# An annealed emission order with convolution taps on GpSimd, in a kernel of linear attention and a gated convolution FFN

## The chip, the cores and the metric

One core of one Trainium2 chip. The time is the device time of one execution in microseconds (us), the median of several runs; the profiled span is the part of it that the trace covers. PE is TensorE's matmuls, PEld its weight loads, DVE is VectorE, ACT ScalarE, POOL GpSimd, SP the engine that here only issues transfers.

## The reference

```python
batch, n_heads, seq, head_dim = (8, 8, 576, 64)      # d_model 512, d_ff 1024, kernel 3
kv = np.einsum('bhsd,bhse->bhde', k, v)
out = np.einsum('bhsd,bhde->bhse', q, kv)
x = out / np.sqrt(np.mean(out * out, axis=-1, keepdims=True) + 1e-06) * g_norm   # -> (B, S, 512)
h = np.maximum(x @ w_in, 0.0)                        # (B, S, 1024)
conv = sum(conv_w[k] * shifted(h, k) for k in range(3))   # depthwise along the sequence
y = (h * sigmoid(conv)) @ w_out
```

## The kernel before

All work is described as a list of small operations with their dependences. The program, before it emits anything, simulates this list with 250 random perturbations and emits the best order found. The batches are handled in five groups, `(0,), (1,), (2, 3), (4, 5), (6, 7)`. The FFN has the layout (channel on partitions, sequence on the free axis); a "tap" multiplies one row of channels of h by a factor that differs per partition, a column of `cw_rel`; an "edge" copies the first column of each sequence, on ACT; an "add" adds shifted taps, on DVE; a "gate" multiplies h by the sigmoid.

```python
def tap(j, ...):                                   # j = 0: left neighbour, 2: right one
    nc.vector.tensor_scalar_mul(
        cst["t"][:, f - f0, :], g.h[:, f, :], cw_rel[:, j, f:f + 1])
def edge(...):                                     # first column of each sequence
    nc.scalar.activation(cv[:, :, :1], hv[:, :, :1], AX.Copy)
def add(j, ...):                                   # three tensor_adds on DVE: conv = h + shifted tap,
    ...                                            # then conv += shifted second tap
def sigmoid(f, ...):
    nc.scalar.activation(cst["c"][:, f - f0, :], cst["c"][:, f - f0, :], AX.Sigmoid,
                         scale=cw_rel[:, 1, f:f + 1])
def gate(...):
    nc.vector.tensor_mul(hs, hs, cst["c"])
...
t0.append(plan.op("DVE", t_cost, tap, 0, deps=relu + t0[:1] + [ratio_done]))
ed = plan.op("ACT", 0.25, edge, deps=h_all)
a0 = plan.op("DVE", a_cost, add, 0, deps=t0 + [ed])
t2 = [plan.op("DVE", t_cost, tap, 2, deps=[a0]) for tap, _ in taps]
a2 = plan.op("DVE", a_cost, add, 1, deps=t2)
Hold(r_tap, t0[0], [a2])          # one tap tile: taps, add, taps, add, one after the other
```

Only batch 0 has its convolution on PE, as matmuls with diagonal matrices (`C_PE = (1, 0, 0, 0, 0)`).

The loads are issued by GpSimd: batch 0 in two halves, w_in, batch 1, w_out, then k, v and q of each later batch, each once its buffer (two batches back) is free. The results leave on SP's queue through `outp = pool("outp", 3)`, three output tiles.

Of the kernel before, what the change touches and what calls it, by code (L numbers as in the profile page):

```python
# [64 lines left out]

BY_ACT = (1, 1, 1, 0, 0)
Q_DMA = (0, 0, 0, 0, 0)
R_DMA = (0, 0, 0, 1, 1)
C_PE = (1, 0, 0, 0, 0)
NORM_TABLES = "natural_log_exp_and_others"  # L70
NF = 4
# [7 lines left out]

# [4 lines left out]
class Hold:  # L84
    def __init__(self, ring, first, last):
        self.ring, self.first, self.left = ring, first, len(last)
        first.takes.append(self)
        for op in last:
            op.gives.append(self)


class Op:
    def __init__(self, at, engines, cost, fn, args, deps):
        self.at, self.engines, self.cost, self.fn, self.args = at, engines, cost, fn, args
        self.kind = fn.__name__ if fn else ""
        self.deps = sorted({d.at for d in deps})
        self.takes, self.gives, self.users = [], [], set()
        self.group = self.engine = None
        for d in deps:
            d.users.add(at)  # L100


class Plan:
# [4 lines left out]

    HOP = 0.2
    ROUNDS = 250  # L110
# [4 lines left out]
    def op(self, engines, cost, fn, *args, deps=()):  # L115
        engines = engines if isinstance(engines, tuple) else (engines,)
        cost = cost if isinstance(cost, tuple) else (cost,) * len(engines)
        o = Op(len(self.ops), engines, cost, fn, args, deps)
        o.group = self.group
        self.ops.append(o)  # L120
        return o

    def run(self, places, back=False):

        ops, n = self.ops, len(self.ops)
        deps = [sorted(o.users) for o in ops] if back else [o.deps for o in ops]
        users = [o.deps for o in ops] if back else [sorted(o.users) for o in ops]
        left = [len(d) for d in deps]
        free, held = {}, {}
        if not back:  # L130
            for o in ops:
                for h in o.gives:
                    held[h], free[h.ring] = h.left, h.ring.free
        ready = sorted((places[i], i) for i in range(n) if not left[i])
        busy, end, eng, order = {}, [0.0] * n, [None] * n, []
        events, waiting = [0.0], []
        while events:
            now = heapq.heappop(events)
            while waiting and waiting[0][0] <= now + 1e-6:
                _, i, kind = heapq.heappop(waiting)  # L140
                if kind:
                    bisect.insort(ready, (places[i], i))
                    continue
                if not back:
                    for h in ops[i].gives:
                        held[h] -= 1
                        free[h.ring] += held[h] == 0
                for u in users[i]:
                    left[u] -= 1
                    if not left[u]:  # L150
                        at = max([now] + [end[d] + (0.0 if eng[d] in ops[u].engines else self.HOP)
                                          for d in deps[u]])
                        heapq.heappush(waiting, (at, u, 1))
                        heapq.heappush(events, at)
            started = []
            for item in ready:
                o = ops[item[1]]
                e = next((e for e in o.engines
                          if e == "LAND" or busy.get(e, 0.0) <= now + 1e-6), None)
                if e is None or not back and any(free[h.ring] < 1 for h in o.takes):  # L160
                    continue
                if not back:
                    for h in o.takes:
                        free[h.ring] -= 1
                end[o.at] = busy[e] = now + o.cost[o.engines.index(e)]
                eng[o.at] = e
                order.append(o.at)
                started.append(item)
                heapq.heappush(waiting, (end[o.at], o.at, 0))
                heapq.heappush(events, end[o.at])  # L170
            for item in started:
                ready.remove(item)
        return (max(end) if len(order) == n else float("inf")), end, eng, order

    def passes(self, places, count):
        best = (float("inf"),)
        for _ in range(count):
            got = self.run(places)
            if got[0] < best[0]:
                best = got  # L180
            if got[0] == float("inf"):
                break
            span, end, _, _ = self.run([-e for e in got[1]], back=True)
            places = [span - e for e in end]
        return best

    def order(self):
        ops = self.ops
        way = [0.0] * len(ops)
        for o in reversed(ops):  # L190
            way[o.at] = min(o.cost) + self.HOP + max((way[u] for u in o.users), default=0.0)
        best = self.passes([-w for w in way], 8)
        rnd = random.Random(1)
        for _ in range(self.ROUNDS):
            width = rnd.choice((1, 2, 4, 8))
            each, shift = rnd.random() < 0.7, {}
            places = [e - min(o.cost) + (rnd.gauss(0, width) if each else
                                    shift.setdefault((o.group, o.kind), rnd.gauss(0, width)))
                      for o, e in zip(ops, best[1])]
            got = self.passes(places, 2)  # L200
            if got[0] <= best[0]:
                best = got
        for o, e in zip(ops, best[2]):
            o.engine = e
        return [ops[i] for i in best[3]]


class Group:
    def __init__(self, n, bs, S):
        self.n, self.bs, self.G, self.T = n, bs, len(bs), S * len(bs)  # L210
        self.kv, self.qT, self.sq = {}, {}, {}
        self.n_o = 0
# [3 lines left out]
def kernel(  # L216
# [53 lines left out]
    for lo in (0, H // 2):  # L270
        for name, src in (("k", k), ("v", v), ("q", q)):
            load(0, name, src, lo, lo + H // 2)
            if lo == 0 and name == "v":
                make_identity(nc, ident)
    w_in_sb = consts.tile([P, n_hd, D_ff], BF16, name="w_in_sb")
    for fs in (slice(0, D_ff // 2), slice(D_ff // 2, D_ff)):
# [3 lines left out]
    def load_batch(b):  # L280
        for name, src in (("k", k), ("v", v), ("q", q)):
            load(b, name, src)

    load_batch(1)
    w_out_sb = consts.tile([P, n_ff, D_model], BF16, name="w_out_sb")
    nc.gpsimd.dma_start(out=w_out_sb, in_=moe_w_out.rearrange("(f p) m -> p f m", p=P))
# [26 lines left out]

    rows = ident.rearrange("p (t m) -> p t m", m=SM)
    neg = consts.tile([P, 2], FP32, name="neg")
    for w in range(2):
        nc.vector.tensor_reduce(neg[:, w:w + 1], rows[:, :, 8 * (w + 1):], mybir.AxisListType.XY,
                                AL.add, negate=True)

# [19 lines left out]

    def dve(n, rate):  # L340
        return 0.16 + n * rate * 0.00104
# [10 lines left out]
    def product(g, bi, t):  # L352

        ps = two_banks("ot_ps")
        for i in range(2):
# [9 lines left out]
    def attention(g):  # L365
# [3 lines left out]
        for bi, b in enumerate(g.bs):  # L369
            kv_done, free_k, free_q = [], [], []  # L370
            hs = H // 2 if first else H
            outs, tr_done, trs = [], None, []
            for h0 in range(0, H, hs):
                st = {}

                def kv_mm(bi=bi, b=b, h0=h0, st=st, n=hs // 2):
                    k_sb, v_sb = qkv["k", b], qkv["v", b]
                    st["ps"] = ps = one_bank([P, n, D], FP32, "kv_ps")
                    for hp in range(n):
                        for r in range(R):  # L380
                            for i in range(2):
                                h = h0 + 2 * hp + i
                                nc.tensor.matmul(  # L383
                                    ps[i * D:(i + 1) * D, hp, :],
                                    k_sb[:, h, r * D:(r + 1) * D], v_sb[:, h, r * D:(r + 1) * D],
                                    start=(r == 0), stop=(r == R - 1))

                def kv_out(bi=bi, h0=h0, st=st, n=hs // 2):
                    if h0 == 0:

                        g.kv[bi] = attn.tile([P, n_hd, 2, D], BF16, name="kv_sb", bufs=6)
                    for i in range(2):
                        for half in range(2):
                            dst = g.kv[bi][half * D:(half + 1) * D, h0 // 2:h0 // 2 + n, i, :]
                            move(st["op"], dst, st["ps"][i * D:(i + 1) * D, :, :])

                mm = plan.op("PE", 1.35 * hs / H, kv_mm,
                             deps=[loaded["k", b, h0], loaded["v", b, h0]] + g.need_kv[bi])
                st["op"] = ev = plan.op(EITHER, 4 * act(hs * 32), kv_out, deps=[mm] + kv_done[:1])
# [3 lines left out]
                if g.by_dma:  # L403
# [5 lines left out]
                    t_issue = plan.op("SP", 1.0, tr, deps=[loaded["q", b, h0]] + g.need_qT[bi])  # L409
                    tr_done = plan.op("DMA", 4.5, None, deps=[t_issue])  # L410
# [466 lines left out]
```

## Time and profile before

| | before |
|---|---|
| time, median of 4 runs (with the changed kernel) | 219.26 us (218.53 to 220.64) |
| profiled span, mean granted PE clock | 215.6 us, 0.971 |
| 1152-element taps on DVE | 48 of 532 ns |
| first h matmul, first output matmul | 23.3 us, 54.8 us |

The busy shares, the clock, the DMA row and the windows are shown in the prediction. Two more lines are needed. First the page's chain that ended last, the share of the span by engine; the chain of before ends where it meets an unbroken run of PE, so it explains only the last 60 us:

```profile
PE 26%; ACT 1%; issue 0%; DVE 0%; ACTq 0%
```

Second, two groups by form (operation, partitions x elements, count, busy us, mean ns of one). The first is the DVE tap; the second is the only one-input arithmetic that GpSimd did in this kernel, in fp32, a step of a Newton iteration:

```profile
L670 DVE TENSOR_SCALAR tap<-h,cw_rel 128x1152 bf16<-128x1152 bf16 x48 | 23.8, 532 | 5.6 <-ACT h L621 4.6
...
L496 POOL TENSOR_SCALAR tmp<-tmp 128x288 f32<-128x288 f32 x6 | 4.0, 662 | 0.5
```

### The profile page before, as it was taken

To read this page: it belongs to the slowest core of one execution; us is meant where nothing else is said; L and a number is where in the kernel's file an instruction comes from. 1 tells how busy PE (TensorE), PEld (TensorE's weight loads), DVE (VectorE), ACT (ScalarE), POOL (GpSimd) and SP (SyncE) were. 2 spreads that over 40 slices of the span, in tenths; PEclk is the share of its full clock that TensorE was granted. 3 is DMA by queue.
4 is the path that set the end of the run, shared out by engine and by line. 5 is a ranking of instruction groups with operands and counts; after the bars stand their busy time and mean duration, and the time that the engine had idled before them with its cause. 6 is when DMAs were issued, how large, how long until landed. Compare 5 with 4: busy or idle time off the path is not lost. (4 is left out here: it accounts for less than half of the span.)

```text
span 215.6 us, 4371 instructions
## 1 busy us (share of the span) xinstructions
PE 182.1 (84%) x1742; PEld 111.4 (52%) x1753; DVE 153.2 (71%) x266; ACT 145.5 (68%) x235; POOL 43.1 (20%) x60
## 2 busy tenths in 40 slices
PE   1363898969999697997999999498899999997991
PEld 0341475757657433685554677253447765443440
DVE  2096527688789769867988699999969899972000
ACT  2274169887798969579994468849469798744331
POOL 7841021122120310980003840000000000000000
PEclk9999999999999759999999999889999999999997
DMA  4999999999999999122994108911552101554553
GB/s 61 192 205 205 204 206 204 204 203 205 202 225 224 204 204 210 33 73 82 216 235 135 27 27 201 220 21 49 144 148 61 41 1 51 146 146 128 153 155 99
DMA packets 31575, 30.99 MB, mean 144 GB/s; under 512 B 2092, under 2 KB 26948, under 8 KB 31556
## 3 DMA queue, kind: packets, MB, share of 16 engines
q0 software_dynamic: 20960, 16.25, 48.7%
q1 hardware_dynamic: 10596, 14.47, 26.4%
q8 instruction: 13, 0.21, 0.4%
q14 instruction: 6, 0.05, 0.1%
HBM read 37.24 MB, written 9.73 MB: 218 GB/s over the span
## 5 line engine op out<-in xcount | busy, mean ns | idle before, releaser
L610 PE MATMUL h_ps<-xT,w_in_sb 128*128 128x288 bf16 x512 | 70.8, 295 | 4.2 <-ACT h L621 3.3
L734 PE MATMUL o_ps<-w_out_sb,h 128*128 128x512 bf16 (+1 forms) x285 | 68.2, 386 | 4.2 <-ACT o_sb L346 1.2
L610 PEld LDWEIGHTS <-w_in_sb 128*128 128x128 bf16 x512 | 50.4, 101 | 20.9 <-issue 5.6
L621 ACT ACTIVATE h<-h_ps 128x576 bf16<-128x576 f32 x52 | 33.3, 649 | 23.7 <-PE h_ps L610 23.3
L734 PEld LDWEIGHTS <-h 128*128 128x128 bf16 (+1 forms) x296 | 28.4, 100 | 37.6 <-issue 5.6
L346 ACT ACTIVATE o_sb<-o_ps 128x512 f32<-128x512 f32 (+1 forms) x34 | 20.2, 596 | 24.9 <-PE o_ps L734 22.1
L696 ACT ACTIVATE conv<-conv,cw_rel 128x1152 bf16<-128x1152 bf16 (+1 forms) x32 | 34.4, 1128 | 0.2
L670 DVE TENSOR_SCALAR tap<-h,cw_rel 128x1152 bf16<-128x1152 bf16 (+1 forms) x64 | 29.4, 495 | 5.7 <-ACT h L621 4.6
L444 ACT ACTIVATE sq<-ot_ps 128x576 bf16<-128x576 f32 x32 | 19.7, 653 | 5.0 <-PE ot_ps L358 3.7
L701 DVE TENSOR_TENSOR h<-h,conv 128x1152 bf16<-128x1152 bf16 (+2 forms) x15 | 21.4, 1434 | 2.0 <-ACT conv L696 1.8
L691 DVE TENSOR_TENSOR conv<-h,tap 128x1152 bf16<-128x1152 bf16 (+8 forms) x33 | 20.8, 683 | 0.3
L693 DVE TENSOR_TENSOR conv<-conv,tap 128x1152 bf16<-128x1152 bf16 (+8 forms) x33 | 20.1, 665 | 1.0
L422 PE MATMUL qT_ps<-ident,q_sb 96*128 96x96 bf16 x192 | 13.8, 222 | 4.3 <-ACT kv_sb L346 2.3
L346 ACT ACTIVATE kv_sb<-kv_ps 64x256 bf16<-64x256 f32 (+1 forms) x32 | 11.2, 351 | 8.8 <-PE kv_ps L383 8.5
L348 DVE COPY qT<-qT_ps 128x576 bf16<-128x576 bf16 x20 | 8.8, 454 | 10.9 <-PE qT_ps L422 10.8
L358 PE MATMUL ot_ps<-qT,kv_sb 64*64 64x288 bf16 x192 | 14.2, 318 | 1.9 <-ACT sq L444 0.9
L549 DVE SCALAR_TENSOR_TENSOR xT<-ot_ps,g_sb,rb 128x576 bf16<-128x576 f32 x16 | 12.8, 813 | 4.0 <-PE ot_ps L358 3.8
L623 DVE TENSOR_SCALAR h<-h_ps 128x576 bf16<-128x576 f32 x12 | 9.0, 755 | 8.0 <-PE h_ps L610 7.9
L422 PEld LDWEIGHTS <-q_sb 96*128 96x128 bf16 x192 | 10.9, 106 | 7.1 <-issue 3.1
L581 DVE TENSOR_TENSOR xT<-o,rb_ps 128x576 bf16<-128x576 f32 x16 | 11.2, 747 | 2.6 <-PE rb_ps L573 2.6
L383 PE MATMUL kv_ps<-v_sb,k_sb 96*64 96x64 bf16 x384 | 8.9, 208 | 4.3 <-DMA v_sb<-in_v_dram 4.3
L264 POOL DMA_DIRECT2D k_sb<-in_k_dram x9 | 7.0, 780 | 25.5 <-PE kv_ps L383 19.6
(61 smaller groups left out, 132.6 us busy)
## 6 DMA issues: line engine op xcount, KB each, us to landing
out_dram<-o_sb SPq DMA_DIRECT2D x24, 192.0 KB, 2.3
rb<-scr SPq DMA_DIRECT2D x16, 288.0 KB, 6.6
k_sb<-in_k_dram POOLq DMA_DIRECT2D x7, 576.0 KB, 13.9
v_sb<-in_v_dram POOLq DMA_DIRECT2D x7, 576.0 KB, 16.0
q_sb<-in_q_dram POOLq DMA_DIRECT2D x7, 576.0 KB, 15.7
out_dram<-o_sb SPq DMA_DIRECT2D x24, 128.0 KB, 2.3
out_dram<-o_sb SPq DMA_DIRECT2D x24, 64.0 KB, 2.0
w_in_sb<-in_moe_w_in_dram POOLq DMA_DIRECT2D x2, 512.0 KB, 11.6
```

The costliest lines, as they stand in the source:

```text
L346: nc.scalar.activation(dst, src, AX.Copy, scale=1.0 if scale is None else scale)
L358: nc.tensor.matmul(ps[i * D:(i + 1) * D, e, :HS], g.kv[bi][es, t, i, :], g.qT[bi][es, 2 * t + i, :], start=True, stop=True)
L422: nc.tensor.transpose(ps[:, i, j * PS:(j + 1) * PS], q_sb[:, 2 * t + i, j * P:(j + 1) * P], ident[:PS, :PS])
L444: nc.scalar.activation(g.sq[bi, t], ust["ps"][:, :, :HS], AX.Square)
L610: nc.tensor.matmul(ps[:, e, :HS], w_in_sb[:, t, f * P:(f + 1) * P], g.xT[:, t, at:at + HS], start=(t == 0), stop=(t == n_hd - 1))
L621: nc.scalar.activation(dst, st["ps"][:, :, :HS], AX.Relu)
L670: nc.vector.tensor_scalar_mul(cst["t"][:, f - f0, :], g.h[:, f, :], cw_rel[:, j, f:f + 1])
L691: nc.vector.tensor_add(c[:, :, here], h[:, :, here], t[:, :, there])
L693: nc.vector.tensor_add(c[:, :, there], c[:, :, there], t[:, :, here])
L696: nc.scalar.activation(cst["c"][:, f - f0, :], cst["c"][:, f - f0, :], AX.Sigmoid, scale=cw_rel[:, 1, f:f + 1])
L701: nc.vector.tensor_mul(hs, hs, cst["c"])
L734: nc.tensor.matmul(st["ps"][:n, :], g.h[:, f, t0:t0 + n], w_out_sb[:, f, :], start=(f == 0), stop=(f == n_ff - 1))
```

## The change

The intent: replace the search in the program by a list found by annealing outside (operation number, engine as a letter: `a` ACT, `d` DVE, `p` GpSimd; `*n` adds n matmuls that only keep the clock warm), let that search place the taps on GpSimd too, bring batch 0 in faster, and take work off PE.

```diff
-Q_DMA = (0, 0, 0, 0, 0)
-C_PE = (1, 0, 0, 0, 0)
+Q_DMA = (0, 0, 0, 0, 1)              # q of batches 6, 7 transposed by DMA
+C_PE = ((0, 0, 0, 0), (0, 0), ...)   # no convolution on PE
+TAPS = ("DVE", "POOL")
+PARTS = (3, 1)                       # batch 0: three head pairs, then one
+ORDER = """
+    122 8 7 4 6 5 14*5 15a 16 0 9 26 ... 57p 59 60p 219 61d 69d ... 84p 379 85p ...
+    ... (685 entries)
+"""
 ...
     def order(self):
-        ...                           # 250 rounds of simulation
+        for entry in ORDER.split():
+            entry, _, fill = entry.partition("*")
+            o = self.ops[int(entry.rstrip("adp"))]
+            o.engine = {"a": "ACT", "d": "DVE", "p": "POOL"}.get(entry[-1], o.engine)
+            o.fill = int(fill or 0)
+            yield o
 ...
-                    nc.vector.tensor_scalar_mul(
+                    eng = nc.gpsimd if cst[j, f].engine == "POOL" else nc.vector
+                    eng.tensor_scalar_mul(
                         cst["t"][:, f - f0, :], g.h[:, f, :], cw_rel[:, j, f:f + 1])
 ...
-                nc.scalar.activation(cv[:, :, :1], hv[:, :, :1], AX.Copy)
+                nc.gpsimd.tensor_copy(cv[:, :, :1], hv[:, :, :1])
 ...
-            t_cost = dve(g.T, 0.25)
+            t_cost = 0.215 + g.T * 0.00026
 ...
+                cst[0, f] = op = plan.op(TAPS, (t_cost, 2.3 * t_cost)[:len(TAPS)], tap, 0,
+                                         deps=relu + t0[:1] + [ratio_done])
```

Cut here: the fp32 spread matrix of batch 0's normalization (`spread32`), the kv matmuls of the other order, loads of w_in and w_out in halves placed by the list (w_in now after batch 1, w_out after batch 5), and `tails`, which writes the two 64-row output tiles of batches 0 and 1 into one. The search's price for a tap on GpSimd: 2.3 times DVE's, which is 2.3 x (0.215 + 1152 x 0.00026) = 1.18 us at 1152 elements.

## The prediction

> **What bounds the kernel now.** I read the page's busy shares first, then the chain that ended last, then a table of windows, and last the timeline where PE loses time. Busy shares do not decide it: no engine is full.
>
> ```profile
> PE 182.1 (84%) x1742; PEld 111.4 (52%) x1753; DVE 153.2 (71%) x266; ACT 145.5 (68%) x235; POOL 43.1 (20%) x60
> ...
> PEclk9999999999999759999999999889999999999997
> DMA  4999999999999999122994108911552101554553
> ```
>
> The chain gives the price of PE's work. It runs back over 60 us through PE alone, and matmuls stand end to end there, so a duration divided by its count is a true rate:
>
> ```profile
> 162.87 11.76 PE h_ps L610 x96
> ...
> 178.32 1.73 PE o_ps L734 x8
> 180.04 0.98 PE h_ps L610 x8
> ...
> 194.84 1.25 ACT conv L696
> ...
> 196.12 0.77 DVE h L701
> ```
>
> So an h matmul (288 columns) costs 0.1225 us and an o matmul (512 columns) 0.216 us; the last two lines are the one hole of the tail, the wait for the last sigmoid and gate. At such rates all matmuls (the small ones priced by columns, kv as 48 in 0.79 us, four "product" matmuls as 0.14 us) come to about 156 us; the span is 215.6. PE is the bound, but 60 us of the span are not its work: some 20 at the start, 4.4 after the last matmul, and the rest are losses between. The windows tell where (columns: PE, PEld, DVE, ACT, POOL busy, clock, DMA share, GB/s):
>
> ```profile
> 26.00:70.00 44.00, 40.71 (x608) 29.36 (x606) 31.57 (x59) 35.85 (x60) 8.73 (x12) 1.00 1.30 209
> 70.00:85.00 15.00, 12.07 (x117) 5.65 (x112) 11.45 (x26) 13.13 (x24) 2.81 (x4) 0.77 1.31 204
> 85.00:130.00 45.00, 42.72 (x457) 28.11 (x459) 36.67 (x52) 32.23 (x55) 19.67 (x24) 1.00 0.44 106
> 130.00:145.00 15.00, 11.91 (x82) 8.33 (x82) 14.79 (x20) 11.24 (x16) 0.00 (x0) 0.89 0.73 158
> 145.00:190.00 45.00, 43.62 (x275) 24.54 (x277) 41.02 (x66) 35.10 (x50) 0.00 (x0) 1.00 0.29 78
> ```
>
> Until about 86 us the loads saturate the DMA queue (share over 1, 205 GB/s, the nines of the DMA row). Pricing the matmuls that start in each stretch, PE does 32 us of work in 26 to 70 (0.72 per us, though busy 93%), 7 in the 15 us of the second row, 39 in the third, 10 in the fourth, 42 in the fifth. After 70 us 117 us of work take 141: 24 lost. Of these the clock took 0.23 x 15 + 0.11 x 15 = 5.1, the tail's hole 2.6, and one stall 2.9:
>
> ```profile
> 132.67 4.69 ACT L696 ACTIVATE conv<-conv,cw_rel 128x1152 bf16<-128x1152 bf16 x4
> ...
> 137.95 5.75 PE L610 MATMUL h_ps<-xT,w_in_sb 128*128 128x288 bf16 x32 [2.93 <-ACT h L621]
> ```
>
> Four sigmoids in a row keep ACT from the relu that empties PSUM. The other 13 us are many short waits, DVE being 82 to 99% busy there.
>
> **What the Trainium skill says.** "SBUF — State Buffer", section "Who interferes with whom": VectorE and GpSimd share a port pair under an exclusive lock; a DVE operation in a two-port mode, or with two SBUF inputs against a GpSimd operation that reads SBUF, and the GpSimd operation block each other, whichever is second waiting. The trace agrees: GpSimd's tensor_tensor takes 0.79 us at the median and 1.79 at most, both long ones under a DVE operation of two SBUF inputs, and a DVE tap of 0.53 us took 1.07 at 93.49 us, while GpSimd multiplied. "GPSIMD Engine Reference", section "Engine selection": one-input elementwise work is roughly at line rate there. The trace has only fp32 of 288 elements, 0.433 us at the least. "TensorE: Matmul & The Clock Gate", Part 1: the clock is halved after an idle window of about 3.4 us and restored by sustained work. The trace shows slow matmuls at the start (four h matmuls in 1.12 us at 23.3, eight in 1.14 later); the half clock at 73 us came with PE busy, which this does not explain, so I can't rule it out after the change.
>
> **The change part by part.** I compared the order of instructions on each engine in both builds.
> 1. Convolution of batch 0 leaves PE: 64 matmuls, 13,808 columns, at 0.1225 / 288 per column = 5.9 us off PE. Three diag builds (3.5 us) leave DVE. In their place: 16 more taps, and 24 adds of batch 0, 8 x (0.455 + 0.352 + 0.253) = 8.5 us on DVE; ACT sigmoids are 8 x 0.12 longer.
> 2. The two half-filled output tiles of batches 0 and 1 become one in two column halves: 8 x 0.216 = 1.7 us off PE if the halves run side by side.
> 3. q of the last two batches is transposed by DMA: 48 PE transposes at about 0.043 = 2.1 us off PE, 8 copies of 0.45 = 3.6 us off DVE. It happens long before it is needed.
> 4. Batch 0 is normalized in parts (three head pairs, then one), with an fp32 spread: no split (1.7 us on DVE), but fp32 matmuls at an estimated 0.5 us each, 8 of them, and 10 filling matmuls to warm the clock. All this is before 26 us, where PE was busy 10.6 of 21 us: no cost, but also little gain, since w_in is now loaded after batch 1. By the 2.95 us that each 576 KB load takes at 205 GB/s: batch 0 at 14.3, batch 1 at 23, w_in at 26 and 31. The first h matmul moves from 23.3 to about 26; batch 1 comes 5 us sooner.
> 5. w_out is now loaded after batch 5: 14.3 + 15 x 2.95 + 2 x 2.7 + 5.1 = 69 us. The first output matmul moves from 54.8 to about 69; by then PE does all h of batches 0 and 1 and attention up to batch 5, 29 us of work in 43, the rate of before.
> 6. 38 of 80 taps go to GpSimd, with the edge copies (2.5 us off ACT). DVE saves 19 x 0.53 + 19 x 0.38 = 17 us of them. GpSimd at about 1.15 ns an element (0.433 less 0.1 fixed, over 288) takes 19 x 0.76 + 19 x 1.42 = 41 us beside DVE. Some two thirds of DVE's time then is lock-taking work (taps, adds, gates), so I put the waits at 0.4 us a tap, 15 us: DVE's saving is nearly all given back.
> 7. ACT: three table loads fewer (3.9 us), 5 relus, 2 scalings, 3 evictions and several kv copies fewer: about 14 us off.
> 8. The order: PE's runs are fewer (119 groups against 151), and ACT's late sigmoids stand one or two at a time between relus, not by fours.
>
> Sum for PE: -9.7 us after 26 us, of which the convolution's share lies before 70. At 69 us the new order still has 115 us ahead (288 full o matmuls 62.3, 384 h 47.0, small ones 6), where before had 117 at 70. So the first 70 us gain 1 to 2 us, and the rest must come from the losses. Of 24 us I expect 17: clock 4, tail's hole 3, no sigmoid stall, short waits 10 by the better order, lock waits included. 69 + 115 + 17 + 4.4 = 205.5 us of span. Timed runs were 1.019 times the profiled span (219.6 / 215.6): 209; I say 208, ACT's relief added.
>
> **The rivals.** (a) The lock wins: each tap on GpSimd holds up an add or a gate for a microsecond, DVE (already 99% busy in 130 to 145) becomes the bound with 108 us of own work after 70 plus 20 to 30 of waits, and little is left: 215 to 220. For it: the stretched operations above. Against: many DVE operations there read PSUM and need no lock, and the short taps are early. (b) The late w_out starves PE: GpSimd both issues loads and runs taps in order, so a tap waiting for a relu delays a load; each us of DMA gap before 69 moves the end by one: 212 to 216. Against: most loads are issued a load or two ahead. (c) The order works as found, small waits fall to 5 us and the clock holds: 198 to 202. (d) The kv matmuls now do six on one column half before the other; if they no longer pair, seven batches cost up to 0.5 us more each, 3 us, mostly before 70.
>
> **Range and chances.** (c) sets the low end, (b) with part of (a) the high one: 200 to 217, middle 208. Under 215.2 is faster by over 2%: 0.83. Within 2%: 0.14, if the lock or the loads take all. Slower: 0.03.
>
> **What would show it.** Right: no c_ps group; first o_ps at 66 to 71 us; DMA nines unbroken until about 86; PE busy some 170; DVE busy 155 to 170, adds and gates longer than before (1.38 and 2.55 us at full size); GpSimd busy about 85; ACT about 131; no PE wait over 2 us on a relu after 100. Wrong: the chain running through DVE adds or GpSimd taps (rival a), DMA gaps before 70 (b), or a second long half-clock stretch.

## The result, and the profile after

| | before | after |
|---|---|---|
| time, median of 4 runs | 219.26 us (218.53 to 220.64) | 274.37 us (272.72 to 275.52) |
| ratio, 95% interval | | 1.250 (1.241 to 1.259) |
| profiled span, mean PE clock | 215.6 us, 0.971 | 273.7 us, 0.869 |
| first h matmul, first output matmul | 23.3, 54.8 us | 30.6, 89.4 us |

The changed kernel is 25% slower. A ratio, here and below, is the mean time of one kernel's fast runs over that of the other's in the same rounds, so not quite the ratio of the medians quoted. The sets of runs were not all on the same chip, and the kernel before had medians from 217.98 to 220.33 us in them; ratios are compared, not times of different sets.

The changed kernel's page: busy us and share of each engine, then the clock, the DMA engines' busy tenths and their GB/s in 40 slices (of 6.8 us here), then the chain by engine:

```profile
PE 203.0 (74%) x1696; PEld 118.6 (43%) x1707; DVE 165.7 (61%) x265; ACT 133.3 (49%) x206; POOL 155.7 (57%) x114
...
PEclk9999998687685699999779999577779977997799
DMA  6999909949999499669540009834000210541255
GB/s 91 203 202 205 149 1 149 198 60 203 174 164 199 91 160 203 112 166 222 143 111 7 0 22 219 205 89 143 0 0 2 77 38 4 148 117 34 83 154 153
...
POOL 31%; DVE 27%; PE 22%; DMA 8%; issue 7%; ACT 2%; DVEq 0%; POOLq 0%; ACTq 0%
```

Every engine but GpSimd has a lower share of busy time than before: nobody is full, and the chain goes through GpSimd and DVE (58% together) instead of PE. The clock drops repeatedly: it was at half speed for 71.7 us in sum, against 12.7 before (2.4 of these after the last matmul). Eight of its ten drops come during or after an idle stretch of PE of 3.1 to 10.8 us; the two at 59 and 66 us come with PE 71% and 84% busy in the 6.8 us before, and stay unexplained. And the DMA engines, which before ran at 205 GB/s almost to 86 us, have a hole at 34 to 41 us (149, 1, 149).

The changed kernel's taps by form (the last part of a line is the idle time of the engine just before, and what ended it):

```profile
L746 POOL TENSOR_SCALAR tap<-h,cw_rel 128x1152 bf16<-128x1152 bf16 x19 | 68.1, 3590 | 41.4 <-DVE conv L769 18.2 <-DVE conv L767 15.3 <-ACT h L695 7.9
L746 POOL TENSOR_SCALAR tap<-h,cw_rel 128x576 bf16<-128x576 bf16 x19 | 35.0, 1845 | 16.0 <-DVE conv L767 12.8 <-DVE conv L769 1.9 <-issue 1.1
...
L746 DVE TENSOR_SCALAR tap<-h,cw_rel 128x1152 bf16<-128x1152 bf16 x29 | 26.7, 953 | 3.0 <-ACT h L695 2.3
```

A tap that takes DVE 0.53 us takes GpSimd 3.59, and the taps left on DVE took longer too, 953 ns in the mean against 532. That mean mixes two kinds: 24 of the 29 took 0.50 to 0.52 us as before, four took 3.46 to 3.47 and one 1.42. The 38 GpSimd taps take 103.1 us. How the two engines hold each other up is in the changed kernel's waits (who waits for whom: sum us, count, longest):

```profile
POOL tap L746 <- DVE conv L767: 28.1, 9, 8.2
...
DVE conv L767 <- POOL tap L746: 23.6, 7, 11.6
DVE conv L769 <- POOL tap L746: 20.7, 9, 6.6
POOL tap L746 <- DVE conv L769: 20.1, 7, 6.8
```

DVE's adds wait 44.3 us for GpSimd's taps, and GpSimd's taps 48.2 us for DVE's adds: since the convolution goes tap, add, tap, add with one tile, the engines take turns rather than work side by side. Where they do work side by side, the timeline shows the lock (start, duration, engine):

```profile
118.72 2.70 DVE L767 TENSOR_TENSOR conv<-h,tap 128x2304 bf16<-128x2304 bf16 x3
121.45 4.32 DVE L746 TENSOR_SCALAR tap<-h,cw_rel 128x1152 bf16<-128x1152 bf16 x3
121.53 3.52 POOL L746 TENSOR_SCALAR tap<-h,cw_rel 128x1152 bf16<-128x1152 bf16 x1 [3.19 <-DVE conv L767]
...
125.88 2.70 DVE L769 TENSOR_TENSOR conv<-conv,tap 128x2304 bf16<-128x2304 bf16 x3
```

Both engines start taps when the first add ends. Three DVE taps would be 1.6 us; they take 4.32, because one of them lasts as long as the GpSimd tap beside it. The whole step takes 4.4 us where four DVE taps would take 2.1. This is what the Trainium skill says in "SBUF — State Buffer", section "Who interferes with whom": the loser of the shared port pair is blocked for the whole instruction. The four long DVE taps above are of this kind.

Two further things changed for the worse. GpSimd's queue is executed in order, and the loads of k, v and q are in it (timeline of GpSimd):

```profile
35.58 0.19 POOL L758 COPY conv<-h 128x2 bf16<-128x2 bf16 x1 [17.66 <-DVE h L697]
35.75 1.73 POOL L746 TENSOR_SCALAR tap<-h,cw_rel 128x576 bf16<-128x576 bf16 x1
...
38.50 1.90 POOL L746 TENSOR_SCALAR tap<-h,cw_rel 128x576 bf16<-128x576 bf16 x1 [1.02 <-DVE conv L767]
40.35 0.83 POOL L237 DMA_DIRECT2D k_sb<-in_k_dram  x1
```

GpSimd's queue stood for 17.66 us at a copy of two columns that waited for a relu, and issued no load in that time: this is the hole in the DMA row. And SP's queue holds the two DMA transposes of q, which wait for the last q loads, with output stores behind them. First the SP queue's own wait, then those that follow from it, all of the changed kernel; before, the largest of this kind was 1.1 us (last fence):

```profile
SPq L409 <- DMA q_sb<-in_q_dram: 16.1, 1, 16.1
```

```profile
PE o_ps L819 <- ACT o_sb L330: 18.0, 4, 10.8
ACT o_sb L330 <- DMA out_dram<-o_sb: 16.8, 3, 11.7
DVE o_sb L332 <- DMA out_dram<-o_sb: 12.7, 3, 7.0
```

```profile
ACT o_sb L346 <- DMA out_dram<-o_sb: 1.1, 1, 1.1
```

### The profile page after: what moved, and what is told of

The parts are those of the page before. It is cut to its first block, busy times and chain, and to the rows that moved or that the text cites. A ratio compares the mean times of both kernels' runs of the same rounds, so it can differ in the third digit from the quotient of the medians.

```text
span 273.7 us, 4338 instructions
## 1 busy us (share of the span) xinstructions
PE 203.0 (74%) x1696; PEld 118.6 (43%) x1707; DVE 165.7 (61%) x265; ACT 133.3 (49%) x206; POOL 155.7 (57%) x114
## 4 chain that ended last, share of the span: by engine, by line
POOL 31%; DVE 27%; PE 22%; DMA 8%; issue 7%; ACT 2%; DVEq 0%; POOLq 0%; ACTq 0%
POOL tap L746 25%; DVE tap L746 8%; DVE conv L767 8%; DVE conv L769 7%; PE o_ps L819 7%; DMA k_sb<-in_k_dram 6%; PE h_ps L684 5%; PE kv_ps L377 3%; PE rb_ps L615 2%; DMA v_sb<-in_v_dram 2%; POOL tmp L526 2%; PE qT_ps L425 2%; POOL tmp L525 2%; POOL rs L528 1%; DVE o L334 1%
## 5 line engine op out<-in xcount | busy, mean ns | idle before, releaser
L746 POOL TENSOR_SCALAR tap<-h,cw_rel 128x576 bf16<-128x576 bf16 (+1 forms) x38 | 103.1, 2718 | 57.4 <-DVE conv L767 28.1
L819 PE MATMUL o_ps<-w_out_sb,h 128*128 128x512 bf16 x269 | 74.5, 429 | 19.2 <-ACT o_sb L330 18.0
L684 PE MATMUL h_ps<-xT,w_in_sb 128*128 128x288 bf16 x512 | 75.2, 308 | 14.2 <-ACT h L695 8.2
L772 ACT ACTIVATE conv<-conv,cw_rel 128x1152 bf16<-128x1152 bf16 (+1 forms) x40 | 41.4, 1058 | 29.8 <-DVE conv L769 29.7
L819 PEld LDWEIGHTS <-h 128*128 128x128 bf16 x280 | 29.4, 108 | 58.8 <-issue 35.4
L330 ACT ACTIVATE o_sb<-o_ps 128x512 f32<-128x512 f32 x31 | 18.2, 592 | 47.2 <-PE o_ps L819 28.0
L767 DVE TENSOR_TENSOR conv<-h,tap 128x576 bf16<-128x576 bf16 (+8 forms) x45 | 23.6, 580 | 24.1 <-POOL tap L746 23.6
L769 DVE TENSOR_TENSOR conv<-conv,tap 128x576 bf16<-128x576 bf16 (+8 forms) x45 | 25.0, 610 | 21.3 <-POOL tap L746 20.7
L758 POOL COPY conv<-h 128x2 bf16<-128x2 bf16 (+2 forms) x15 | 4.7, 314 | 23.3 <-DVE h L697 21.2
L377 PEld LDWEIGHTS <-k_sb 96*64 96x64 bf16 x432 | 11.9, 142 | 12.4 <-DMA k_sb<-in_k_dram 7.3
L639 DVE SCALAR_TENSOR_TENSOR xT<-ot_ps,g_sb,rb 128x576 bf16<-128x576 f32 x16 | 12.2, 808 | 1.0 <-PE ot_ps L350 1.0
## 6 DMA issues: line engine op xcount, KB each, us to landing
q_sb<-in_q_dram POOLq DMA_DIRECT2D x7, 576.0 KB, 10.8
```

The lines of the kernel that those rows point to most:

```text
L330: nc.scalar.activation(dst, src, AX.Copy, scale=1.0 if scale is None else scale)
L377: nc.tensor.matmul(ps[half * D:(half + 1) * D, hp, i * (halves - 1), :], k_sb[:, h, r * D:(r + 1) * D], v_sb[:, h, r * D:(r + 1) * D], sta ...
L684: nc.tensor.matmul(ps[:, e, :HS], w_in_sb[:, t, f * P:(f + 1) * P], g.xT[:, t, at:at + HS], start=(t == 0), stop=(t == n_hd - 1))
L746: eng.tensor_scalar_mul(cst["t"][:, f - f0, :], g.h[:, f, :], cw_rel[:, j, f:f + 1])
L767: nc.vector.tensor_add(c[:, :, here], h[:, :, here], t[:, :, there])
L769: nc.vector.tensor_add(c[:, :, there], c[:, :, there], t[:, :, here])
```

## The experiments

Theories about the extra 55 us. The tap itself may be slow on GpSimd: because bf16 is (S), or because its factor is a column and not a constant (P). Or the tap is fast and the lock holds it up (L). Beside the taps: the in-order queue of GpSimd delays loads, the transposes delay the stores, the late weights starve PE, or the convolution of batch 0 was better on PE. All kernels gave correct results unless said; four timed runs each unless said.

### All taps back on DVE, and half of them

`d_taps_dve` is the changed kernel with every tap on DVE, at the same place in the list. `e_taps_early` and `e_taps_late` leave the first 19 (576 elements) or the last 19 (1152) on GpSimd.

```diff
-    ... 57p 59 60p ... 84p 379 85p ...
+    ... 57d 59 60d ... 84d 379 85d ...
```

> The changed kernel with all 80 taps on VectorE, in the same places of the same order; the edge copies stay on GpSimd. Theory T (the taps on GpSimd are the cause: 1.71 us for 576 elements and 3.20 for 1152 when nothing disturbs them, in the serial path tap, add, tap, add, sigmoid, gate): the 55 us lost come back and the time is what the rest of the change is worth, 203 to 215 us. Rival O (the listed order, with the late output weights and rigid engine order, is what loses, and GpSimd's taps only show in the chain because all else waits too): 240 us or more.

> Only the 19 early taps (576 elements, batches 0 and 1) on GpSimd, the 19 late ones on VectorE. Theory T with a pure sum of times (19 x 1.71 = 33 us early, 19 x 3.20 = 61 late) says the early ones cost about a third of the loss: 20 us over the kernel with none, some 228. If the early ones matter more because they hold the loads behind them (the DMA gaps at 34 to 41 and 49 to 57 us), more: 235 to 245. Rival O: no different from the full change, 274.

> Only the 19 late taps (1152 elements) on GpSimd. Theory T by the sum: two thirds of the loss, about 245 us; by the chain of the late stage alone (the taps on GpSimd on it, 19 x 3.2 less the 0.53 each would take on VectorE = 51, of which part is hidden): 235 to 250. Rival O: 274.

| | time (range) | ratio to before (95%) |
|---|---|---|
| `d_taps_dve` | 224.46 (222.81 to 226.31; the profiled run, the longest, was slow) | 1.025 (1.015 to 1.035) |
| `e_taps_early` | 233.78 (232.99 to 234.19) | 1.070 (1.063 to 1.077) |
| `e_taps_late` | 263.72 (262.42 to 265.29) | 1.207 (1.194 to 1.219) |

So taps on GpSimd cost some 49 us of the 55 ((1.250 - 1.025) x 219), and the rest of the change, without them, is still 2.5% slower than before. By the ratios the two halves add up: 9.8 + 39.8 = 49.6 us over `d_taps_dve`. They are not alike: an early tap has 1.71 - 0.37 us more to do than on DVE, 25 us for 19, of which 9.8 show; a late one 3.20 - 0.53, 51 us, of which 39.8 show. So a microsecond of tap costs about 0.4 us early and 0.8 late; whether size or place makes this difference was not separated. None of the three times lies in the range that theory T gave (203 to 215, about 228, 235 to 250): the rest of the change was worth less, and the late taps cost more, than expected. Readings from the profile of `d_taps_dve`, here and below, are of that slow run.

### The same taps on GpSimd in the old kernel

`b_half_taps_pool` is the kernel before with 32 of its 64 taps on GpSimd (8 of 576 elements, 24 of 1152), nothing else:

```diff
-                    nc.vector.tensor_scalar_mul(
+                    eng = nc.gpsimd if (f + j // 2) % 2 == 0 else nc.vector
+                    eng.tensor_scalar_mul(
```

> The kernel before with one thing changed: 32 of its 64 taps (8 of 576, 24 of 1152 elements) on GpSimd, in their places of the old order. Theory T: the loss follows the taps, not the order: 8 x 1.71 + 24 x 3.20 = 90 us of GpSimd work in a serial path, 255 to 290 us. Rival O: the old order hides them, under 230.

274.71 us (273.06 to 275.22), ratio 1.256 (1.247 to 1.265): the same loss without anything else of the change. By form:

```profile
L671 POOL TENSOR_SCALAR tap<-h,cw_rel 128x1152 bf16<-128x1152 bf16 x24 | 85.0, 3547 | 50.0 <-DVE conv L692 23.2 <-ACT h L621 11.2 <-DVE conv L694 11.0
L671 DVE TENSOR_SCALAR tap<-h,cw_rel 128x1152 bf16<-128x1152 bf16 x24 | 36.2, 1524 | 6.7 <-ACT h L621 6.1
```

Here the taps of a step alternate between the engines, so that most DVE taps stand beside a GpSimd tap, and their mean is almost three times that of before. The annealed order is not what made the taps expensive.

### What GpSimd's forms cost alone

`m_pool_forms` is not this kernel: it runs GpSimd operations alone, three times each, with DVE idle. Its output is wrong, which doesn't matter for the time. "ptr" has a factor per partition, "imm" two constants, "tt" two tensors; bf or ff at the start is the type, the number the elements.

```python
nc.gpsimd.tensor_scalar_mul(o, hb[:, :n], sc[:, 0:1])                            # ptr
nc.gpsimd.tensor_scalar(o, hb[:, :1152], -0.5, 1.5, op0=AL.mult, op1=AL.add)     # imm
```

> Measures only (the result is wrong on purpose): the tap on GpSimd alone, VectorE idle, at 288, 576, 1152 and 2304 bf16 elements, and other forms beside it. Theory S (the form itself is slow: bf16 in and out cost about 2.57 ns an element and 0.23 us fixed, as the undisturbed taps of the changed kernel show): 0.97, 1.71, 3.20, 6.16 us with nothing else running, and fp32 in and out at 288 about 0.4 to 0.5 us whether the factor is a constant or a column. Rival P (the factor read from a column of SBUF is what is slow, bf16 or not): fp32 with a column as slow as bf16, bf16 with constants near 1.4 us at 1152. Rival L (the slowness is the port lock): all short here, 1.4 us at 1152.

Its groups by form (count, busy us, mean ns):

```profile
L89 POOL TENSOR_SCALAR bfptr1152r<-hb,sc 128x1152 bf16<-128x1152 bf16 x3 | 9.6, 3192 | 0.0
L92 POOL TENSOR_SCALAR ffptr1152r<-hf,sc 128x1152 f32<-128x1152 f32 x3 | 9.6, 3192 | 0.0
L102 POOL TENSOR_TENSOR fftt1152r<-hf 128x1152 f32<-128x1152 f32 x3 | 6.3, 2097 | 0.0
L94 POOL TENSOR_SCALAR bfimmr<-hb 128x1152 bf16<-128x1152 bf16 x3 | 3.4, 1145 | 0.0
L97 POOL TENSOR_SCALAR ffimm1152r<-hf 128x1152 f32<-128x1152 f32 x3 | 3.4, 1143 | 0.0
L99 POOL COPY bfcopyr<-hb 128x1152 bf16<-128x1152 bf16 x3 | 3.4, 1134 | 0.0
...
L92 POOL TENSOR_SCALAR ffptr288r<-hf,sc 128x288 f32<-128x288 f32 x3 | 3.0, 997 | 0.0
...
L97 POOL TENSOR_SCALAR ffimm288r<-hf 128x288 f32<-128x288 f32 x3 | 1.3, 424 | 0.0
```

The type makes no difference (3192 ns in bf16 and fp32). The form does: 3.19 us with a column against 1.14 with constants. In 576 elements the column form takes 1.71 us (the first of the three bf16 ones 1.86), so one element more costs (3.19 - 1.71) / 576 = 2.57 ns. S falls. L falls as the main cause, since this is without any work on DVE; of the mean of 3.59 us in the changed kernel, 0.40 at most is the lock's. P holds, with one reserve: the column form does one operation (multiply) and the constant form two (multiply, add), and no run has a multiplication by one constant. What is shown is the price of this form against that one; that the column is the reason is the likely reading.

### The changed kernel with constants in place of the column

`c_taps_const` gives the 38 GpSimd taps the form with two constants in place of the column, and changes nothing else. Its output is wrong, which doesn't matter for the time. (Relative error 0.19.)

```diff
                     eng = nc.gpsimd if cst[j, f].engine == "POOL" else nc.vector
+                    if eng is nc.gpsimd:
+                        eng.tensor_scalar(cst["t"][:, f - f0, :], g.h[:, f, :], 0.5, 0.0,
+                                          op0=AL.mult, op1=AL.add)
+                        return
                     eng.tensor_scalar_mul(
                         cst["t"][:, f - f0, :], g.h[:, f, :], cw_rel[:, j, f:f + 1])
```

> The changed kernel as it is, with one edit: the 38 taps on GpSimd multiply by the constant 0.5 and add 0 in place of the factor from a column of SBUF (wrong result on purpose). Alone, that form took 1.14 us at 1152 elements where the column form took 3.19. The prediction's step 6 priced these taps at 0.76 and 1.42 us. Theory C (the price of the column form is the whole error of the forecast): 203 to 212 us. Rival W (lock waits and loads delayed behind taps and edge copies in GpSimd's queue cost much even with fast taps): 218 to 235 us. The run with no tap on GpSimd took 224.5.

232.48 us (230.08 to 235.75, one run slow), ratio 1.061 (1.051 to 1.071). By ratios, the column form alone cost (1.250 - 1.061) x 219 = 41 us. The group by form and the largest wait:

```profile
L748 POOL TENSOR_SCALAR tap<-h 128x1152 bf16<-128x1152 bf16 x19 | 29.0, 1539 | 42.3 <-DVE conv L772 18.1 <-ACT h L696 10.0 <-DVE conv L774 9.8
```

```profile
POOL tap L748 <- DVE conv L772: 39.7, 11, 9.2
```

Theory C (203 to 212 us) fails and rival W (218 to 235) holds. A tap at 1.54 us is close to the 1.42 predicted, and still GpSimd waits for the adds, and the kernel is 8 us slower than with all taps on DVE (1.061 against 1.025). Even at the price that the search believed in, this placement does not pay. Those 8 us hold the lock (DVE's 1152-element taps take 750 ns in the mean here), the turns of tap and add, and loads held up in the queue; they were not separated.

### The edge copies and the old order of loads

`f_edges_act` is `d_taps_dve` with the edge copies back on ACT; `h_loads_old` is that with w_in and w_out loaded as before (w_in ahead of batch 1, w_out after it).

```diff
-                nc.gpsimd.tensor_copy(cv[:, :, :1], hv[:, :, :1])
+                nc.scalar.activation(cv[:, :, :1], hv[:, :, :1], AX.Copy)
-            ed = plan.op("POOL", 0.25, edge, deps=h_all)
+            ed = plan.op("ACT", 0.25, edge, deps=h_all)
```

> The changed kernel with all taps on VectorE and the 15 edge copies on ScalarE as before, in the same places of the order. Theory E (with the taps gone, what still delays the loads is that the edge copies wait for their relus in GpSimd's queue ahead of the load issues: DMA fell to 24 GB/s at 34 to 39 us): no gap in the DMA row before 85 us, first output matmul some 8 to 10 us earlier, time 212 to 218 us. Rival Q (the two DMA transposes on the SP queue, which wait for the last q loads while output stores wait behind them): 220 us or more still, with the stall of the stores at about 86 to 127 us still there. If both hold, the loads come earlier and so do the transposes.

> The same with the loads issued in the old order: w_in before batch 1, w_out after batch 1, the rest unchanged. The list expects w_out late, so its engines will wait for batches 2 to 5 where it has them early. If the late w_out was what holds PE: 3 to 8 us under the run with edges on ScalarE. If the load order was right for this list: 3 to 8 us over it.

| | time (range) | ratio to before (95%) |
|---|---|---|
| `f_edges_act` | 219.75 (218.74 to 219.98) | 1.004 (0.996 to 1.011) |
| `h_loads_old` | 221.86 (221.68 to 223.88) | 1.017 (1.010 to 1.024) |

Copies of 0.19 us cost 4.7 us ((1.025 - 1.004) x 219), for what they wait for in an in-order queue. The 219.75 us lie between theory E and rival Q: the early gap went, a later one stayed. In `d_taps_dve`, GpSimd's largest waits and its timeline where the hole was:

```profile
POOL conv L728 <- DVE h L747: 44.3, 7, 10.1
POOL conv L728 <- ACT h L665: 42.6, 4, 20.6
```

```profile
35.57 0.19 POOL L728 COPY conv<-h 128x2 bf16<-128x2 bf16 x1 [17.56 <-ACT sq L418]
36.05 0.77 POOL L207 DMA_DIRECT2D k_sb<-in_k_dram  x1 [0.29 <-issue]
```

In `f_edges_act` a q load is issued at 30.18 us, then v and k, and the DMA row's early hole is gone; the next one, 14 GB/s in the slice from 43.6 us, stays:

```profile
GB/s 65 201 202 204 204 205 203 205 14 149 204 203 206 204 204 204 217 169 58 110 230 218 100 48 3 119 218 222 146 144 0 30 114 27 122 115 178 96 201 135
```

The late weights were not a mistake: the old order of loads is about 1.3% slower in this list (2.9 us, where 3 to 8 were expected). With a fixed list this is not quite fair to the old order, as the list was annealed for the new one.

### The convolution of batch 0

`b_conv_dve` is the kernel before, with its own search, and batch 0's convolution on DVE. `g_conv_pe` is `f_edges_act` with it on PE: the convolution matmuls and their sigmoid where the sigmoid was, the diagonal matrices built again, the list renumbered.

```diff
-C_PE = (1, 0, 0, 0, 0)                                   # b_conv_dve
+C_PE = (0, 0, 0, 0, 0)
-    diag_done = [plan.op("DVE", 1.3, cw_diag, j, deps=[cw_done]) for j in range(3)]
+    diag_done = []
```

> The kernel before with its own search, batch 0's convolution on VectorE instead of PE, and no diag matrices. By the prediction's step 1: 5.9 us off PE, 3.5 off VectorE, some 14 on (16 taps of 0.38, 24 adds for 8.5 us), all before 70 us, where PE did 0.72 us of work per us: 214 to 220 us, so -2 to 0% against before. If VectorE was the hidden limit there: 220 to 226.

> The changed order with all taps on VectorE, edge copies on ScalarE and batch 0's convolution back on PE (conv matmul and its sigmoid together at the place of the old sigmoid, diag built again). The old search lost 4.4% when this convolution moved to VectorE. Theory V (VectorE, not PE, is short of time at 26 to 70 us, so moving the convolution off PE was a loss and not the gain of step 1): 2 to 5 us under the run with edges on ScalarE (219.75): 214 to 218. Rival: PE is short, 222 to 226.

`b_conv_dve` took 228.13 us (228.07 to 228.61), ratio 1.044 (1.038 to 1.050): step 1 of the prediction, done alone, loses 4.4%. The search then finds another order, whose clock is 0.916, so the edit and the order are not separated, and both expectations (214 to 220, 220 to 226) were missed. `g_conv_pe` took 221.77 us (220.56 to 222.99), ratio 1.016 (1.008 to 1.024), against 1.004 for the same list with the convolution on DVE, run in another set. The two intervals overlap, and neither expectation was met, so that the step is worth about a per cent in the new list is suggested and not shown; in the old search, with its new order, it is harmful. Its value depends on the order around it.

### More output tiles, and the order of three loads

`o_six_stores` is `f_edges_act` with six output tiles, so that evictions need not wait for stores behind the transposes. `q_loads_kv` is that, and k and v of batches 4 and 5 are loaded ahead of q of the same batch: in the list `381 ... 380 ... 379` (q, v, k) became `380 379 381`. `r_conv_pe_kv` is `g_conv_pe` with this order of loads and four output tiles (six did not fit into SBUF beside the diagonal matrices: that kernel, `p_conv_pe_six`, failed to build). `b_four_stores` is the control, the kernel before with four output tiles.

```diff
-    outp = pool("outp", 3)
+    outp = pool("outp", 6)          # o, q; 4 in r and in the control
```

> The run with all taps on VectorE and edges on ScalarE, with six output tiles instead of three. There output evictions waited 22 us in all for stores that stand behind the two DMA transposes and the norm broadcasts on the SP queue, and PE waited 4.6 + 3.3 us for those evictions. Theory: PE gets those 8 us back, and with them perhaps a half-clock stretch (3.4 us at 121): 210 to 215 us. Rival: the waits are filled otherwise, 217 to 220.

> The run with six output tiles, with one edit to the list: for batches 4 and 5 the k and v loads are issued ahead of the q load, not behind it. There the q load of batch 4 waits up to 15 us in GpSimd's queue for the transposes of batch 2's q, v and k wait behind it, and the DMA row falls to 48 GB/s at 43 to 53 us. Theory (a load that waits for its buffer holds up others in the in-order queue): the gap shrinks, 210 to 214 us. Rival (VectorE, 83% busy at 26 to 70 us, sets the pace there): 215 to 217, no change.

> The same load order, with batch 0's convolution on PE and four output tiles (six do not fit beside diag). If relief of VectorE and of the loads add up: 208 to 213 us, the best of the study; if PE is the bound after 85 us in any case: 214 to 218.

> Control: the kernel before, order unchanged, with four output tiles in place of three. It has no DMA transposes in the SP queue, and its evictions waited 1.1 us for stores: 217 to 220 us, same. If it gains 3 to 4 us as the changed order did, the gain of the run with six was not due to the transposes.

| | time (range) | ratio to before (95%) |
|---|---|---|
| `o_six_stores` | 215.91 (215.37 to 216.41) | 0.989 (0.982 to 0.995) |
| `q_loads_kv` | 215.70 (215.08 to 216.04) | 0.977 (0.973 to 0.981) |
| `r_conv_pe_kv` | 219.55 (218.64 to 220.63) | 0.995 (0.990 to 1.000) |
| `b_four_stores` | 218.27 (217.67 to 219.51) | 0.988 (0.983 to 0.993) |

In `f_edges_act` the transposes did hold up the stores, and through the evictions PE (waits; then the timeline of SP's queue, where the two transposes take 13.07 us from the first issue to the end of the second):

```profile
ACT o_sb L331 <- DMA out_dram<-o_sb: 10.4, 4, 3.4
...
PE o_ps L820 <- ACT o_sb L331: 4.6, 2, 2.7
```

```profile
84.73 13.07 SPq L410 DMA_TRANSPOSE qT<-q_sb  x2
```

By the ratios of two sets, six tiles gained 1.5% over `f_edges_act`; 215.91 us lies between the two expectations. But the control gained 1.2% in the kernel before, which has no transposes, so the gain cannot be put down to the transposes: more tiles help either way. Whether `q_loads_kv` is better than `o_six_stores` is not settled, the two times being equal to 0.2 us in sets whose kernel before differed by 2 us. It did close most of the DMA hole (its DMA row has 155 GB/s where `f_edges_act` had 14). `q_loads_kv` beats both kernels, by 2.3% over the one before, and within its own set it also beats the control and `r_conv_pe_kv`. Its time is the one that the rival named (215 to 217), though the hole closed as the theory said; `r_conv_pe_kv` was slower than either of its expectations.

### Does VectorE bound the best version?

In `q_loads_kv` the chain that ended last runs 42% through DVE. `s_relus_act` moves nine relus of batches 2 to 7 from DVE to ACT (five rounds, six runs).

```diff
-    ... 293d 303d ... 297d ... 299d ... 451d ... 489d ... 447d ... 449d ... 587d ...
+    ... 293a 303a ... 297a ... 299a ... 451a ... 489a ... 447a ... 449a ... 587a ...
```

> The run with k and v loads first, with one edit: the nine relus of batches 2 to 7 that the list gives to VectorE go to ScalarE (0.65 us each there, 0.75 on VectorE), in their places. In that run VectorE is busy 43.84 of 45 us at 145 to 190 and 14.86 of 15 at 130 to 145, ScalarE 32.8 of 45. Theory D (the list was made for taps on GpSimd; with them on VectorE it is VectorE that sets the pace after 110 us, which is why the order stays 7 us over the forecast): 9 x 0.75 = 6.8 us off VectorE, of which most shows: 209 to 213 us. Rival (PE's own work and the wait for the last gate set it): 214 to 217.

218.93 us (218.33 to 219.21), ratio 1.003 (0.997 to 1.008), slower than both expectations: by the ratios 5.6 us slower than `q_loads_kv`, by the times of the two sets 3, and not faster. The windows (start:end, length, then PE, PEld, DVE, ACT, POOL busy us, clock, DMA share, GB/s), first of `q_loads_kv`, then of `s_relus_act`, and a wait of the latter:

```profile
130.00:145.00 15.00, 14.38 (x101) 9.75 (x100) 14.86 (x19) 10.15 (x17) 3.62 (x3) 1.00 0.55 126
```

```profile
130.00:145.00 15.00, 12.90 (x95) 9.06 (x93) 11.81 (x13) 11.68 (x17) 4.56 (x4) 1.00 0.51 114
```

```profile
PE h_ps L685 <- ACT h L696: 3.5, 5, 1.8
```

DVE was relieved, 14.86 to 11.81 us of 15, but PE then did less there, and in the whole run waited 3.5 us for the relus on ACT, against 0.6 in `q_loads_kv`. So a chain that runs through DVE did not mean that less work on DVE is a gain; what bounds the best version in its middle stays open.

## Why the prediction was wrong

The prediction said 208 us (200 to 217) and gave "slower" three chances in a hundred; it was 274.

- **Step 6, GpSimd's taps: wrong, and the main failure.** The term "0.76 us and 1.42 us a tap, 41 us beside DVE" measured 1.85 and 3.59 us, 103.1 us in all. The working took 0.433 us from an fp32 operation of 288 elements with *constants* as factors, and scaled it by elements. For that form the scaling was even a little dear (0.424 us at 288 and 1.143 at 1152 in `m_pool_forms`); carrying it over to another form was the error. A column as factor costs 2.57 ns an element, 2.8 times as much at 1152. The prediction looked at the type and the size, and not at the third operand. The sentence in "GPSIMD Engine Reference", section "Engine selection", that one-input work is roughly at line rate, fits the copy and the constant form (1.13 and 1.14 us) and not this one. The search in the change made the same error: its 1.18 us is the constant form's price, and `c_taps_const` shows what the other form cost, 41 us.
- **Step 6, the lock: about the right size, but for taps.** Predicted were 15 us. The 29 DVE taps of 1152 elements grew by 29 x (953 - 532) ns = 12.2 us, not by 0.4 us each but in five that stood long; the adds hardly grew (at 2304 elements the first 1354 ns, 1384 before, the second 1472, 1358 before), and the largest gates by 0.26 us each, of which `d_taps_dve`, without GpSimd taps, has 0.14. An add waits for the taps of its own step, so it rarely stands beside one.
- **Rival (a) in kind, far beyond its size.** "The chain running through DVE adds or GpSimd taps" was named as what would show the prediction wrong, and that is what the page shows (58%). The rival put the loss at a microsecond a tap of the lock; what it did not have is that tap and add alternate, so that a slow tap is not beside DVE's work but in its path. It was priced as engine time beside the rest, and it was a serial chain: 76 us of extra tap time (19 x (3.20 - 0.53) + 19 x (1.71 - 0.37)) turned into some 49 us of span.
- **Rival (b) happened as well.** GpSimd's in-order queue delayed the loads: a hole at 34 to 41 us, w_out issued at 74.8 us, the first output matmul at 89.4 instead of 69 (step 5). Without GpSimd's taps it was at 82.4, with the edges on ACT too at 80.8. There w_out had landed by 74.5 us (issued at 54.9), and PE reached the output matmul in its own order only after it had waited 4.2 us for DVE at 70.4; so step 5 was too early even without taps on GpSimd. The expectation that "most loads are issued a load or two ahead" failed at the copies, which the prediction only counted as 2.5 us off ACT; they cost 4.7 us. Matmuls priced as in the prediction (an estimate), PE had about 124 us of work left at 70 us, where the prediction had 115 at 69; before had 117.
- **Step 3, the transposes by DMA: "long before it is needed" was wrong.** They were issued at 94.6 and 113.8 us, each holding SP's queue for 3.03 us, the second after a wait of 16.1 us for its load, with stores behind them.
- **Step 4: the right order of things, too short.** The first h matmul came at 30.6, not 26. The fp32 spread took 16 records of 682 ns between 20.0 and 28.7 us, two records for each of 8 matmuls: some 1.1 us each at the slow rate of the start rather than 0.5, that is 3.9 times a bf16 matmul of the same columns at that rate (the prediction's four in 1.12 us).
- **Step 8 and the clock: the losses grew.** Of 24 us lost, 17 were to stay (clock 4, tail 3, short waits 10) and 7 to be regained. Instead half-clock time rose from 12.7 to 71.7 us. "TensorE: Matmul & The Clock Gate", Part 1, says that the clock halves after an idle window; eight of the ten drops agree. The long idling followed mostly from the taps: without them, in the same order, the clock is 0.939 to 0.954 (`d_taps_dve`), with the edges on ACT too 0.957 to 0.969 (`f_edges_act`), and in the changed kernel 0.869.
- **Two slips of the sums, both small.** 1.019 divides the time of some executions by the span of another, which itself took 217.7 us (1.010, so 207.5 instead of 209); and 69 + 115 + 17 + 4.4 is 205.4.
- **Right:** no convolution on PE, and PE's priced work lower by about 6 us (an estimate by the prediction's prices; 9.7 were to go, and the fp32 matmuls came); the merged output tile's halves run side by side (step 2; 16 half matmuls in 1.98 us in `f_edges_act`, where eight took 1.89 before); ACT's busy time, 133.3 against 131; DVE's, 165.7 in 155 to 170 (in part by luck, as the waits in it stood elsewhere than predicted); and rival (d), the kv matmuls unpaired, did not occur (48 at full clock in 1.03 us in `d_taps_dve`, 0.95 before). They were right about busy time and said little about the end, because the end was set by waits.

By ratios, times 219 us, the way from the best version to the changed kernel is: the form with a column in place of constants 41 us, having taps on GpSimd at all 8, edge copies on GpSimd 5, three output tiles instead of six 3 (the kernel before gains likewise), order of k, v and q 2.6 (not settled). With the first three undone, the annealed list is as fast as the old search (1.004).

## What to carry to other kernels

Before moving work to another engine, time that very form there (operation, type, size, and whether its scalar is a constant or a column), alone, in a small kernel; a neighbour form in the profile can be off by a factor of 2.8, and a search is only as good as that price. Ask next whether the moved operation stands beside the old engine's work or in series with it: in this chain of tap, add, tap, add, 76 us more of taps put some 49 us into the span. And keep an engine whose in-order queue issues the loads free of work that waits for other engines, however short that work is.

## What the Trainium skill lacked or had wrong

- "GPSIMD Engine Reference", "Engine selection": one-input work is not one class. With constants or as a copy, 1.14 and 1.13 us at 128 x 1152; with a factor per partition, 3.19 us in bf16 and in fp32, slower than a two-tensor multiplication in fp32 (2.10 us). DVE does the bf16 tap in 0.53.
- "SBUF — State Buffer", "Who interferes with whom": agrees (a DVE tap of 0.53 us took 3.47 beside a GpSimd tap). What it lacks is the combination with the above: the slower the GpSimd instruction, the longer each fast DVE instruction stands, 1524 ns in the mean in `b_half_taps_pool`.
- "DMA: Bandwidth & Descriptors", "DMA Transpose (X-bar)": it says which engines may issue a transpose, but its only figures for what an issue takes stand in a comparison made for another chip, under "previous generations". Here one took from 3.0 us (changed kernel) to 8.65 us (`e_taps_late`) on SP's queue, with the stores behind it waiting, also while it waited for its load (16.1 us in the changed kernel).
- No page that I read warns that a 0.19 us copy in the queue that issues the loads can hold them for 17.6 us.
